# A two-stage kernel whose three compute engines keep the program's order, with time mixing placed by hand between the products and fewer PSUM banks for each use

## The chip, the cores and the metric

The kernel runs on one core of one Trainium2 chip. The core has a matrix engine (TensorE, PE in the profile), a vector engine (VectorE, DVE), a scalar engine (ScalarE, ACT), a general engine (GpSimd, POOL) and a queue that issues the loads and stores (SyncE, SP). Each takes its instructions in the order of its own queue and waits at an instruction whose inputs or buffers are not ready. The metric is the device time of one execution in microseconds (us); the lower, the better.

## The reference

An attention block with a decaying state for 4 batches, 8 heads, 768 steps and 48 features a head, and then a gated feed-forward block on its 3072 x 384 output:

```python
for t in range(S):
    kt, vt, rt = (k[:, :, t], v[:, :, t], r[:, :, t])
    cur = np.einsum('bhd,bhe->bhde', u[None] * kt, vt)
    y[:, :, t] = np.einsum('bhd,bhde->bhe', rt, state + cur)
    state = w[None, :, :, None] * state + np.einsum('bhd,bhe->bhde', kt, vt)
...
rms = np.sqrt(np.mean(x * x, axis=-1, keepdims=True) + 1e-06)
xn = x / rms * rms_g
g = xn @ w_gate
silu = g * (1.0 / (1.0 + np.exp(-g)))
val = xn @ w_val
return (silu * val @ w_out).astype(np.float32)
```

d_model is 384 and d_ff is 1536; inputs are float32, the weights arrive as 64-bit words.

## The kernel before, in words

The 768 steps are cut into 12 chunks (`s`) of 64 steps; a chunk holds 256 tokens, 64 of each batch. Two kinds of work are done for every chunk.

**Time mixing** (lines 290 to 423) computes the attention of one chunk from the state that the chunk before left. In the order of `mixing(s)`: `prep_r` scales r and k by the tables of powers of w on DVE (ME from chan, then chan itself) and copies half of ME to MO on ACT. `prep_u` multiplies r, k and u and sums them to `du` on DVE (three instructions on TOK). `diagonal(s, half)` writes `du` times a diagonal mask into ME and MO: 16 small ACT instructions for a half, two DVE instructions for chunk 0 (lines 315 to 328). `prep_k` makes KH on DVE and then issues the next chunk's TOK load. `scores(s, half)` is 16 small matmuls into `pa` and two masked DVE copies from it; the second half issues the next chunk's chan load. `outputs(s, half)` is 24 small matmuls into `py`, then squares (`sq`) and a scaled copy (`yT`) on ACT. `states(s, half)` is 16 small matmuls into `pu` and four ACT copies into VS, and then the next load of VS. `normalise(s)` is one matmul into `pm`, the square root on ACT (with a load of its function table), the reciprocal on DVE, and two products (`xa`, `xb`) with an ACT copy of each to the other half of the partitions. The last chunk has no `states`.

**The feed-forward block** has a first form for chunks 0 and 1 and a second for the other ten. In the first form (here called the first layer), `gate_val(s, nn)` (line 447) computes one of 12 slices of 128 gate and value columns with two calls of `product`, each six matmuls (line 434), then Silu on ACT and a DVE product give `h`; `add_cell(s, q, j)` (line 465) multiplies three slices with the output weights and adds to a sum. While this runs, the weights are loaded in 24 pieces and rounded from 64-bit words: `round_piece` (line 173) has one ACT instruction, two DVE and one on POOL for each, and three load buffers.

In the second form, two chunks are taken as a pair (`s` = 2, 4, 6, 8, 10). `weight_sums` and `token_sums` make sums and differences (DVE), and `group(s, m)` (line 562) computes two slices for both chunks with seven products instead of eight, in PSUM banks a, b and c, each of two halves; the second product of a pair needs the token sum t2. Six groups make a pair's `h`. `project(s, j)` (line 611) then multiplies with the output weights: four times 12 matmuls, one ACT copy and two stores each.

**The check** (line 538) loads the weights a second time in 48 parts, with one buffer (`again`), and looks on ACT for values that the rounding could not represent: two ACT instructions each (`mag`).

**What sets the order.** The program text interleaves lists of steps with the helper `alongside`: so many time-mixing steps after so many product steps. But the order of the text is only a priority there. The framework's scheduler sorts each engine's instructions by its own estimate of when inputs will be ready, for all five queues. PSUM has eight banks: six for `a`, `b`, `c` (two each), one for time mixing (`at`), one for `po`, the sums of `add_cell` and `project`; chunk 0's mixing borrows a, b and c in turn.

## Time and profile before

| what | us |
|---|---|
| median of three runs | 821.41 |
| lowest of the three | 817.68 |
| the profiled execution | 818.58 |
| its span, first to last instruction | 816.7 |
| PE busy | 684.9 |
| DVE busy | 407.8 |
| ACT busy | 354.1 |
| POOL busy | 47.6 |

The highest of the three runs took 3746.5 us. A table row of the profile reads: line, engine, operation, output<-inputs, shapes, count | busy us in all, mean ns of one | idle time of the engine just before these instructions, and what ended it. A row of waits reads: who waited for whom, us in total, times, the longest. A row of the chain of waits reads: start, duration, what. In a table of stages each engine has its busy time and, in brackets, its instructions; PEclk is the clock that TensorE was granted, as a share of full speed; a matmul in float32 stands in the records as two. A row of the timeline reads: start, duration, engine, line, operation, count.

### The profile page before, as it was taken

What the parts mean: (1) busy time and instruction counts of PE and PEld (TensorE: products, weight loads), DVE (VectorE), ACT (ScalarE), POOL (GpSimd) and SP (SyncE); (2) the same over time, 40 slices, a digit from 0 to 9 for tenths busy, and PEclk for the clock granted to TensorE, in tenths of its full rate; (3) what the DMA queues carried; (4) which work ended last, traced back from release to release, by engine and by line L of the source; (5) the groups of instructions that cost most, each with busy time, mean ns of one, the idle gap of its engine ahead of it and who ended that gap; (6) DMA issues with size and microseconds to landing.
All of it is one profiled execution on the core that took longest, in us unless ns stands there. A gap on an engine that the chain in (4) does not pass through costs nothing.

```text
span 816.7 us, 14933 instructions
## 1 busy us (share of the span) xinstructions
PE 684.9 (84%) x6326; PEld 513.0 (63%) x6326; DVE 407.8 (50%) x575; ACT 354.1 (43%) x955; POOL 47.6 (6%) x40
## 2 busy tenths in 40 slices
PE   2484875887767778799997999997999999999996
PEld 2353653655546556665875766875668877578853
DVE  6999671341354235633656526565437654325510
ACT  3673933853583356235255173273262471321200
POOL 5444220000000000000000000000000000000000
PEclk9887898889898889899998999998999999999999
DMA  8767623353533342023022023210230210000000
GB/s 229 213 196 231 194 70 87 83 142 91 120 114 107 87 112 73 1 51 92 10 41 74 16 44 91 41 44 31 50 92 10 41 35 2 20 20 1 2 21 22
DMA packets 20572, 61.32 MB, mean 75 GB/s; under 512 B 3984, under 2 KB 7056, under 8 KB 19344
## 3 DMA queue, kind: packets, MB, share of 16 engines
q1 hardware_dynamic: 20496, 60.28, 28.0%
q8 instruction: 51, 0.84, 0.4%
q14 instruction: 25, 0.20, 0.1%
HBM read 55.54 MB, written 4.72 MB: 74 GB/s over the span
## 4 chain that ended last, share of the span: by engine, by line
PE 47%; DMA 19%; DVE 14%; ACT 13%; issue 3%; POOL 2%; SPq 0%; ACTq 0%; DVEq 0%; POOLq 0%
PE po L621 18%; PE b L439 10%; PE a L439 6%; PE c L439 6%; DMA again<-in_wka_dram 5%; DMA again<-in_wot_dram 4%; DMA again<-in_wkb_dram 4%; DMA chan<-in_chan_dram 4%; ACT ME L328 3%; PE pa L337 2%; ACT mag L547 2%; DMA TOK<-in_tok_dram 2%; ACT MO L328 1%; DVE rms L418 1%; PE py L361 1%
## 5 line engine op out<-in xcount | busy, mean ns | idle before, releaser
L621 PE MATMUL po<-wo,h 128*128 128x384 f32 x480 | 163.1, 493 | 2.8 <-ACT o L629 2.8
L621 PEld LDWEIGHTS po<-wo,h 128*128 128x128 f32 x480 | 88.6, 190 | 63.3 <-ACT o L629 4.9
L439 PE MATMUL b<-t,wb 64*128 64x256 f32 x360 | 49.1, 407 | 19.3 <-DVE gv L589 19.3
L547 ACT ACTIVATE mag<-again 128x288 f32<-128x288 f32 x48 | 22.2, 463 | 94.7 <-DMA again<-in_wka_dram 34.3
L328 ACT ACTIVATE MO<-dmask,du 64x64 f32<-64x64 f32 x176 | 48.3, 338 | 25.8 <-PE py L366 25.2
L471 PE MATMUL po<-wo,h 128*128 128x384 f32 x96 | 43.5, 590 | 16.6 <-DVE o L476 7.2
L439 PE MATMUL gv<-xa,wa 64*128 64x256 f32 x288 | 47.2, 436 | 11.7 <-ACT MO L328 7.5
L439 PE MATMUL c<-t,s 64*128 64x256 f32 x360 | 49.7, 399 | 8.0 <-DVE gv L604 8.0
L439 PEld LDWEIGHTS b<-t,wb 64*128 64x128 f32 x360 | 37.0, 201 | 25.4 <-DVE gv L589 20.9
L439 PE MATMUL b<-xa,wa 64*128 64x256 f32 x360 | 47.9, 398 | 5.2 <-DVE gv L582 5.0
L439 PE MATMUL a<-xa,wa 64*128 64x256 f32 x360 | 49.3, 389 | 3.5 <-DVE h L595 3.5
L361 PE MATMUL py<-ME,VS 128*64 128x64 f32 x288 | 39.8, 242 | 14.4 <-issue 8.6
L439 PE MATMUL b<-t,s 64*128 64x256 f32 x360 | 49.6, 395 | 0.4 <-DVE t L558 0.4
L629 ACT COPY o<-po 128x384 f32<-128x384 f32 x20 | 9.6, 478 | 92.5 <-PE po L621 83.9
L439 PE MATMUL c<-xb,s 64*128 64x256 f32 x360 | 47.9, 400 | 0.7 <-DVE gv L590 0.5
L439 PEld LDWEIGHTS c<-t,s 64*128 64x128 f32 x360 | 37.7, 197 | 15.1 <-DVE gv L604 9.5
L361 PEld LDWEIGHTS py<-ME,VS 128*64 128x64 f32 x288 | 31.4, 153 | 24.9 <-issue 17.4
L439 PEld LDWEIGHTS gv<-xa,wa 64*128 64x128 f32 x288 | 32.5, 211 | 21.2 <-issue 12.5
L439 PE MATMUL a<-xb,wb 64*128 64x256 f32 x360 | 45.4, 384 | 0.0
L337 PE MATMUL pa<-ME,chan 48*64 48x64 f32 x384 | 31.1, 240 | 16.7 <-DVE MO L342 15.1
L328 ACT ACTIVATE ME<-dmask,du 64x64 f32<-64x64 f32 x176 | 44.8, 331 | 0.6
L589 DVE TENSOR_TENSOR gv<-b,m 128x512 f32<-128x512 f32 x30 | 20.7, 692 | 48.4 <-PE b L439 48.3
(120 smaller groups left out, 1324.2 us busy)
## 6 DMA issues: line engine op xcount, KB each, us to landing
TOK<-in_tok_dram SPq DMA_DIRECT2D x12, 768.0 KB, 5.5
chan<-in_chan_dram SPq DMA_DIRECT2D x24, 384.0 KB, 6.1
VS<-in_vpad_dram SPq DMA_DIRECT2D x24, 336.0 KB, 4.9
raw<-in_wka_dram SPq DMA_DIRECT2D x8, 576.0 KB, 5.3
raw<-in_wkb_dram SPq DMA_DIRECT2D x8, 576.0 KB, 6.1
raw<-in_wot_dram SPq DMA_DIRECT2D x8, 576.0 KB, 4.7
again<-in_wka_dram SPq DMA_DIRECT2D x16, 288.0 KB, 2.7
again<-in_wkb_dram SPq DMA_DIRECT2D x16, 288.0 KB, 2.7
```

The source lines that it names most:

```text
L328: nc.scalar.mul(t[rows, b, p, :], dmask[rows], du[rows, x : x + 1])
L337: nc.tensor.matmul(pa[to, bl, p, :], CH[rows, 1, b, p, :], m[rows, b, p, :], start=True, stop=True, skip_group_check=True,)
L361: nc.tensor.matmul(py[64 * z : 64 * z + 64, i, cols], VS[:, z, b, at : at + L], m[:, b, 3, :], start=True, stop=False, skip_group_check=True,)
L418: nc.vector.reciprocal(rms, rms)
L439: nc.tensor.matmul(ps_[:, z, 0:NT], lhs[rows, cc, :], rhs[rows, cc, :], start=start and cc == 0, stop=cc == CC - 1, skip_group_check=True,)
L471: nc.tensor.matmul(po, h[:, j * P : (j + 1) * P], wo[q][:, o, :], start=o == 0, stop=o == NQ - 1)
L547: nc.scalar.activation(mag, hi, AF.Abs)
L589: nc.vector.tensor_add(gv[:, :, 3], bank["b"][sl], m1)
L621: nc.tensor.matmul(po, h_of[s, m][:, 2 * x + j // 2, at : at + P], wo[i][:, o, :], start=m == 0 and x == 0, stop=m == last and x == 1,)
L629: nc.scalar.copy(osb, po)
```

## The change

1. A small class passes every instruction that `fast` gives to PE, DVE or ACT on with the request that it keep the order of the program; `pe`, `dve` and `act` replace `nc.tensor`, `nc.vector` and `nc.scalar`. SP and POOL are not wrapped. (In the profile of the changed kernel and in its order all of these instructions have the line of the helper, L89.)
2. The steps of time mixing are cut finer, each with a letter: R and K (`decay_r`, `decay_k`), 1, 2, 3 (the three instructions of the bonus), d/D (diagonal, first/second half), a/A (scores), m/M (the masked copies), y/Y (outputs), q (squares), r (`pm` and the root), n (normalise), h/H (KH, one half each; H issues the TOK load), u/U (states). `mix(s, "...")` issues them in the order given.
3. `alongside` is gone: every gate_val, add_cell, rounding and mixing step of the first layer is written out, and in the pairs a table says after which product of which group which steps come. One check stands after the third and one after the sixth product of each group, in all pairs but the first. The weight sums are spread over the first pair's start and its groups; the token sums of a pair come directly after the last normalise.
4. Banks: time mixing has two of its own (`at`), also for chunk 0 and for `ps_wk`. The bank for `po` is gone. gate_val alternates between a and b; add_cell takes c, for both token halves at once; the four projections take a, b, c, b. The tile `o` has two buffers.
5. The first VS load is issued ahead of the first weight pieces; `dmask` is made earlier.

The diff, cut to its core:

```diff
+class InOrder:
+
+
+    def __init__(self, tc, engine):
+        self.tc, self.engine = tc, engine
+
+    def __getattr__(self, name):
+        give = getattr(self.engine, name)
+        return lambda *args, **kwargs: self.tc.keep_in_program_order(give(*args, **kwargs))
...
+    pe, dve, act = (InOrder(tc, engine) for engine in (nc.tensor, nc.vector, nc.scalar))
...
-    ps_at = ctx.enter_context(tc.tile_pool(name="ps_at", bufs=1, space=PSUM))
-    ps_o = ctx.enter_context(tc.tile_pool(name="ps_o", bufs=1, space=PSUM))
+    ps_at = ctx.enter_context(tc.tile_pool(name="ps_at", bufs=2, space=PSUM))
...
+    load_v(0)
     stage()
     stage()
-    load_v(0)
     stage()
...
-    rota = deque("abc")
-
-    def at_tile(shape, name, s):
-
-        if s == 0:
-            rota.rotate(1)
-            return ps_gv.tile(shape, FP32, name=name, tag=rota[0])
+
+    def at_tile(shape, name):
         return ps_at.tile(shape, FP32, name=name, tag="at")
...
+    def decay_r(s):
+
+        dve.tensor_mul(ME, CH[:, 0], free_dims(up, (0, B), (L, HP), (1, L)))
+        act.copy(MO[64:128], ME[64:128])
+
+    def decay_k(s):
+        dve.tensor_mul(CH[:, 1], CH[:, 1], free_dims(down, (0, B), (L, HP), (1, L)))
+
+    def bonus_1(s):
+        dve.tensor_mul(TOK[:, 0], TOK[:, 0], TOK[:, 1])
+
+    def bonus_2(s):
+        dve.tensor_mul(TOK[:, 0], TOK[:, 0], free_dims(utab, (0, B), (D, HP), (1, D)))
+
+    def bonus_3(s):
+
...
+                    act.mul(t[rows, b, p, :], dmask[rows], du[rows, x : x + 1])
+
+    def state_k(s, z):
+
+        if s == NS - 1:
+            return
+        rows = slice(64 - 64 * z, 128 - 64 * z)
+        dve.tensor_mul(KH[rows, z], TOK[rows, 1], free_dims(wk[rows], (0, B), (D, HP), (1, D)))
+        if z == 1:
+            load_tok(s + 1)
+
...
+    def rms(s):
+        pm = at_tile([P, NT], f"pm_{s}")
+        pe.matmul(pm, ones, sq_of[s][:, 0], start=True, stop=True)
+        rms_of[s] = one.tile([P, NT], FP32, name=f"rms_{s}", tag="rms")
+        act.activation(rms_of[s], pm, AF.Sqrt, scale=1.0 / DM, bias=eps)
...
-    h_of, turn = {}, deque("abc")
+    h_of, turn = {}, deque("ab")
...
-    def add_cell(s, q, j):
+    def add_cell(q, s):
 
         rounded(PER_Q * (q + 1))
-        po = ps_o.tile([P, DM], FP32, name=f"po_{s}_{q}_{j}", tag="po")
-        for o in range(NQ):
-            h = h_of[s, q * NQ + o]
-            nc.tensor.matmul(po, h[:, j * P : (j + 1) * P], wo[q][:, o, :], start=o == 0, stop=o == NQ - 1)
+        po = ps_gv.tile([P, 2, 512], FP32, name=f"po_{s}_{q}", tag="c")
+        for j in range(2):
+            for o in range(NQ):
+                h = h_of[s, q * NQ + o]
+                pe.matmul(
+                    po[:, j, 0:DM], h[:, j * P : (j + 1) * P], wo[q][:, o, :], start=o == 0, stop=o == NQ - 1
+                )
         if q == 0:
-            sums[s, j] = work.tile([P, DM], FP32, name=f"o_{s}_{j}", tag="o", bufs=2 * FIRST)
-            nc.scalar.copy(sums[s, j], po)
+            sums[s] = work.tile([P, 2, DM], FP32, name=f"o_{s}", tag="o", bufs=FIRST)
+            act.copy(sums[s], po[:, :, 0:DM])
         else:
-            nc.vector.tensor_add(sums[s, j], po, sums[s, j])
+            dve.tensor_add(sums[s], po[:, :, 0:DM], sums[s])
         if q == WQ - 1:
-            store(sums[s, j], s, j)
-
-    late = deque()
-
-    def cell(q, s):
-        steps = []
-        for o in range(NQ):
-            steps.append(lambda o=o: gate_val(s, q * NQ + o))
-            if late:
-                steps.append(late.popleft())
-        late.extend(lambda j=j: add_cell(s, q, j) for j in range(2))
-        return steps
-
-    def alongside(steps, others, spare=0):
-
-        todo, n = deque(others), len(others)
-        for x, f in enumerate(steps):
+            for j in range(2):
+                store(sums[s][:, j], s, j)
...
+    def mix(s, what):
+
+
+        todo = {
+            "R": decay_r, "K": decay_k, "1": bonus_1, "2": bonus_2, "3": bonus_3, "q": squares, "r": rms,
+            "n": normalise,
+        }
+        halves = {"d": diagonal, "a": scores, "m": masked, "y": outputs, "h": state_k, "u": states}
+        for c in what:
+            if c in todo:
+                todo[c](s)
+            else:
+                halves[c.lower()](s, int(c.isupper()))
+
+    def rounding(k):
+        for _ in range(k):
+            round_piece()
+
+    mix(0, "RK123aAdmyDMY")
+    rounding(2)
+    mix(0, "qr")
+    rounding(2)
+    mix(0, "n")
+    gate_val(0, 0), rounding(1), mix(0, "h")
+    gate_val(0, 1), rounding(1), mix(0, "Hu")
+    gate_val(0, 2), mix(0, "U"), rounding(2)
+    add_cell(0, 0), rounding(2)
+    gate_val(0, 3), mix(1, "12")
+    gate_val(0, 4), mix(1, "3Rd")
+    gate_val(0, 5), mix(1, "K"), rounding(1), mix(1, "aDm"), rounding(1)
+    add_cell(1, 0), mix(1, "AMyY"), rounding(1), mix(1, "qr"), rounding(1), mix(1, "n")
+    gate_val(1, 0), rounding(1), mix(1, "h")
+    gate_val(1, 1), mix(1, "Hu"), rounding(1)
+    gate_val(1, 2), mix(1, "U"), rounding(1)
+    add_cell(0, 1), mix(2, "12")
+    gate_val(1, 3), mix(2, "3Rd")
+    gate_val(1, 4), mix(2, "K")
+    gate_val(1, 5), mix(2, "aDm")
+    add_cell(1, 1), mix(2, "A"), rounding(1), mix(2, "M")
+    gate_val(0, 6), mix(2, "y"), rounding(1)
+    gate_val(0, 7), mix(2, "Y")
+    gate_val(0, 8), mix(2, "q"), rounding(1), mix(2, "r")
+    add_cell(2, 0), mix(2, "n")
+    gate_val(1, 6), mix(2, "hHu"), rounding(1)
+    gate_val(1, 7), mix(2, "U"), rounding(1)
+    gate_val(1, 8), mix(3, "12")
+    add_cell(2, 1), mix(3, "3Rd"), rounding(1)
+    gate_val(0, 9), mix(3, "K"), rounding(1)
+    gate_val(0, 10), mix(3, "aDm")
+    gate_val(0, 11), rounding(1), mix(3, "AM")
...
+    add_cell(3, 0), mix(3, "h")
+    gate_val(1, 9), mix(3, "yH")
+    gate_val(1, 10), mix(3, "Y"), sum_1(0)
+    gate_val(1, 11), mix(3, "q"), sum_2(0), mix(3, "r")
+    add_cell(3, 1), mix(3, "nuU")
+    token_sum(2, 1), token_sum(2, 2)
 
     for s in range(FIRST, NS, 2):
+        first_block, n = s == FIRST, s + 2
+        fill = {}
+        if first_block:
+            fill.update({(0, 0): lambda: (token_sum(s, 3), sum_3(0)), (0, 1): lambda: (token_sum(s, 4), sum_4(0))})
+            fill.update({(1, 0): lambda: sum_1(1), (2, 0): lambda: sum_2(1), (2, 1): lambda: sum_4(1)})
+            fill.update({(2, 4): lambda: sum_3(1)})
+        if n < NS:
+            plan = {
+                (0, 2): "R", (1, 1): "K", (1, 4): "1", (2, 0): "2", (2, 2): "3d", (3, 0): "h", (3, 2): "aDm",
+                (4, 0): "H", (4, 2): "AM", (4, 4): "y", (5, 2): "Y", (5, 4): "q", (5, 5): "u",
+            }
         else:
+            plan = {}
+        for m in range(NN // 2):
+            steps = group(s, m)
+            for k, f in enumerate(steps):
+                f()
+                if (m, k) in fill:
+                    fill[m, k]()
+                if (m, k) in plan:
+                    mix(n, plan[m, k])
+                if not first_block and k in (2, 5):
+                    check()
+        if n == NS:
+            for j in range(4):
+                project(s, j, False), project(s, j, True)
+            break
+        mix(n, "U"), mix(n + 1, "R12")
+        project(s, 0, False), mix(n, "r"), mix(n + 1, "3K")
+        project(s, 0, True), mix(n + 1, "ad"), mix(n, "n")
+        project(s, 1, False), mix(n + 1, "ADmh")
+        project(s, 1, True), mix(n + 1, "yMH")
+        project(s, 2, False), mix(n + 1, "Yq")
+        project(s, 2, True), mix(n + 1, "r")
+        project(s, 3, False), mix(n + 1, "un")
+        project(s, 3, True), mix(n + 1, "U")
+        for x in (1, 2, 3, 4):
+            token_sum(n, x)
...
+    po_of = {}
+
+    def project(s, j, second):
+
+        if not second:
+            po_of[s, j] = ps_gv.tile([P, DM], FP32, name=f"po_{s}_{j}", tag="abcb"[j])
+        po = po_of[s, j]
...
```

More of the change, by code (lines that the diff above doesn't have):

```diff
@@ new lines, in run @@
+    def run(*steps):
+        for f in steps:
+            f()
+    def mix(s, what):
[9 more added lines that the diff above has]
+                halves[c.lower()](s, int(c.isupper()))
@@ L605, in seventh @@
[L605 to L607 removed]
+            dve.tensor_add(gv[:, :, 1], bank["c"][sl], gv[:, :, 1])
+            act.activation(gv[:, 0, 1], gv[:, 0, 1], AF.Silu)
+            dve.tensor_mul(h[:, 2:4], gv[:, 0, 2:4], gv[:, 1, 2:4])
+            dve.tensor_mul(h[:, 1], gv[:, 0, 1], gv[:, 1, 1])
         return [first, second, third, fourth, fifth, sixth, seventh]
[L611 to L632 removed]
@@ new lines, in project @@
+    def project(s, j, second):
+        if not second:
+            po_of[s, j] = ps_gv.tile([P, DM], FP32, name=f"po_{s}_{j}", tag="abcb"[j])
+        po = po_of[s, j]
+        last = NN // 2 - 1
+        for m in range(3, 6) if second else range(3):
+            for x in range(2):
+                i, o = divmod(m + x * NN // 2, NQ)
+                at = (j % 2) * P
+                pe.matmul(
+                    po, h_of[s, m][:, 2 * x + j // 2, at : at + P], wo[i][:, o, :],
+                    start=m == 0 and x == 0, stop=m == last and x == 1,
+                )
+        if second:
+            osb = work.tile([P, DM], FP32, name=f"o_{s}_{j}", tag="o", bufs=FIRST)
+            act.copy(osb, po)
+            store(osb, s + j // 2, j % 2)
```

234 lines of the change are left out of this document (78 added, 156 removed).

## The prediction

> **What bounds the kernel now.** I read the page's head first, then busy time by stage, then what TensorE (PE) waited for in each stage, then the chain of waits and the durations of single instructions.
>
> ```profile
> span 816.7 us, 14933 instructions
> ```
>
> The profiled execution took 818.58 us, so 1.9 us lie around the span. The median of the runs, 821.41, stands 2.8 above it. Busy time by stage, cut where PE's work changes (first product of the first layer at 40.1, its last matmul at 250.2, then each pair of chunks):
>
> ```profile
> core 0: us, PE busy (x) PEld busy (x) DVE busy (x) ACT busy (x) POOL busy (x), PEclk, DMA share, GB/s
> 0.00:40.10 40.10, 12.45 (x231) 11.25 (x231) 31.94 (x59) 19.34 (x52) 19.32 (x21) 0.93 0.83 224
> 40.10:250.20 210.10, 154.39 (x1374) 109.86 (x1375) 112.92 (x141) 118.16 (x326) 28.28 (x19) 0.86 0.48 133
> 250.20:388.30 138.10, 114.03 (x1034) 84.64 (x1034) 58.59 (x85) 62.49 (x181) 0.00 (x0) 0.91 0.28 72
> 388.30:502.10 113.80, 106.42 (x1055) 80.59 (x1054) 60.88 (x85) 49.95 (x136) 0.00 (x0) 0.97 0.19 48
> 502.10:616.85 114.75, 107.60 (x1055) 81.47 (x1054) 60.97 (x85) 50.07 (x136) 0.00 (x0) 0.97 0.19 48
> 616.85:722.25 105.40, 103.53 (x995) 78.25 (x994) 52.96 (x76) 38.91 (x95) 0.00 (x0) 1.00 0.10 23
> 722.25:810.50 88.25, 86.50 (x596) 66.92 (x596) 29.50 (x49) 14.75 (x30) 0.00 (x0) 1.00 0.04 10
> 810.50:816.70 6.20, 0.00 (x0) 0.00 (x0) 0.00 (x0) 0.46 (x1) 0.00 (x0) 0.70 0.15 37
> ```
>
> The late pairs are PE-bound: 103.53 busy in 105.40 at clock 1.00. The loss is early: PE idles 56 us in 40.1 to 250.2 and 24 in the next stage, and its clock there is 0.86 and 0.91. Of the waits, the first three are PE's between 40 and 250, the fourth PE's in the whole run; then what ScalarE (ACT) waited for at the weight check:
>
> ```profile
> PE pa L337 <- DVE MO L342: 15.1, 3, 7.4
> ...
> PE gv L439 <- ACT MO L328: 7.5, 1, 7.5
> ...
> PE pu L395 <- ACT VS L403: 5.6, 2, 3.2
> ```
> ```profile
> PE b L439 <- DVE gv L589: 19.3, 4, 6.4
> ```
> ```profile
> L547 ACT ACTIVATE mag<-again 128x288 f32<-128x288 f32 x48 | 22.2, 463 | 94.7 <-DMA again<-in_wka_dram 34.3 <-DMA again<-in_wot_dram 34.1 <-DMA again<-in_wkb_dram 26.3
> ```
>
> All 48 checks stand early in ACT's queue, with one buffer, and ACT sits 94.7 us in front of a load that starts only when the check before is read. The Silu behind it is late, then VectorE (DVE), then PE.
>
> **The price list.** From the chain of waits (a product, a projection half of six matmuls, the same product after a long idle, the square root's table load and the root); DVE; ACT; DMA landings:
>
> ```profile
> 34.42 1.28 ACT L417
> ...
> 35.72 0.48 ACT rms L417
> ```
> ```profile
> 436.21 4.42 DMA TOK<-in_tok_dram
> ...
> 447.70 2.93 PE b L439 x12
> ...
> 454.87 1.29 PE c L439 x12
> ...
> 462.42 4.07 PE po L621 x12
> ```
> ```profile
> L190 DVE SCALAR_TENSOR_TENSOR bits<-raw,bits 128x576 int32<-128x576 int32 x24 | 25.6, 1068 | 0.5
> L418 DVE RECIPROCAL rms<-rms 128x256 f32<-128x256 f32 x12 | 21.0, 1750 | 20.7 <-ACT rms L417 20.7
> L310 DVE TENSOR_TENSOR KH<-TOK,wk 64x768 f32<-64x768 f32 x22 | 20.9, 952 | 29.6 <-PE pu L395 29.1
> ...
> L295 DVE TENSOR_TENSOR chan<-chan,down 128x1024 f32<-128x1024 f32 x12 | 14.7, 1223 | 29.7 <-DMA chan<-in_chan_dram 29.7
> ...
> L456 DVE TENSOR_TENSOR h<-gv,h 128x256 f32<-128x256 f32 x24 | 10.1, 422 | 66.6 <-ACT h L455 66.5
> ```
> ```profile
> 36.09 3.91 ACT L328 ACTIVATE MO<-dmask,du 64x64 f32<-64x64 f32 x16
> ```
> ```profile
> L294 ACT COPY MO<-ME 64x1024 f32<-64x1024 f32 x12 | 12.5, 1042 | 0.8 <-DVE ME L293 0.4
> ...
> L455 ACT ACTIVATE h<-gv 128x256 f32<-128x256 f32 x24 | 8.9, 371 | 0.7 <-PE gv L439 0.5
> ```
> ```profile
> again<-in_wka_dram SPq DMA_DIRECT2D x16, 288.0 KB, 2.7
> ```
>
> So 16 diagonal multiplies in one piece hold ACT for 3.9 us. ME has chan's shape (1.2); xa, xb and the token sums have KH's columns (0.95); a copy of 768 columns is 0.8 by MO's 1.04 for 1024. A restart after an idle of several us costs 2.93 - 1.29 = 1.64.
>
> **The change, part by part.** First, ACT in the first layer. Before, checks (mag) stand between the Silus (h) of chunk 0:
>
> ```order
> L455 ACTIVATE h_0_785<-gv_0_772 128x256
> L547 ACTIVATE mag_2527<-again_2525 128x288
> L548 ACTIVATE mag_2527,seen<-mag_2527 128x288
> L455 ACTIVATE h_1_822<-gv_1_809 128x256
> L547 ACTIVATE mag_2550<-again_2548 128x288
> ```
>
> After, no check stands there, but a chunk's diagonal is one piece ahead of a Silu:
>
> ```order
> L89 ACTIVATE h_4_534<-gv_4_521 128x256
> L89 COPY MO<-ME 64x1024
> L89 ACTIVATE ME<-dmask,du_537 64x64 x8
> L89 ACTIVATE MO<-dmask,du_537 64x64 x8
> L89 ACTIVATE h_5_570<-gv_5_557 128x256
> ```
>
> What moved: the checks go to the groups of the last four pairs (after products 3 and 6, so 3.9 or 5.2 us apart, against 2.7 for a landing and some 0.6 around it: no wait left), and h_5 now stands behind 16 multiplies. On DVE, `chan<-chan,down` stands behind h_5, and the scores need chan.
>
> Stage 1, to the first product: the same chain, without two KH and the roundings that stood between: 40.1 becomes 38.
>
> Stage 2, the first layer. PE's work at full clock: 24 gate_val of two products, 24 x 2.58 = 62; 8 add_cell, 8 x 4.07 = 33; mixing. One mixing is read from the pair at 616.85: 103.53, less 42 products (54) and 8 halves (33), leaves 16.5 for two that lack one chunk's states, so some 9; three, and chunk 0's states (2), are 29. Sum 124. Its stalls, walked through the new order:
> - scores of chunk 1: ME 1.2, MO 1.0, diagonal 3.9, Silu 0.4, h 0.4, chan 1.2 in a row, 8.1, with one gate_val (2.6) of cover less 2 lost at its start: 7. Chunks 2 and 3 have two gate_vals: 5 each. Sum 17.
> - states: KH (two of 0.95) and a rounding (two steps, the longer 1.07, so up to 2.1) stand on DVE behind h, which itself waits for the Silu: 5, 4, and 7 for chunk 2, whose xa and xb copies and two table loads stand ahead of that Silu. Sum 16.
> - weights just in time: gate_val 3 waits for a raw load issued behind VS (some 5), add_cell 1 for a rounding behind the masks (5). Sum 10.
> - xa of chunk 1 is used at once: squares, pm, 1.28 + 0.48, reciprocal 1.75, two of 0.95, copy 0.8: 7.5. Chunk 2's pm: 1.5. Sum 9.
> - restarts: about nine of these exceed 3 us: 9 x 1.64 = 15.
> That is 67, so 191 in place of 207.5 (to the second layer's first product, 2.6 of which lie before 250.2). Stage 2 ends at 229, before at 247.6. Two banks for gate_val instead of three cost nothing: the bank comes back after two gate_vals, 5.2 us, and Silu and h take 0.8; if a diagonal stands there, it is in the stalls above. add_cell as one tile moves as many columns.
>
> Stage 3, first pair: before 388.3 - 247.6 = 140.7, most of it checks. A full pair's work is 103.5 + 1.9 = 105.4. Added: the second product waits for t2 behind chunk 3's reciprocal (4) and restarts (1.6); eight weight sums in the groups' DVE, 1.4 each by KH's 0.95 for 768 columns of their 1152, of which I leave 2.5 uncovered; the diagonal (below). Sum 115.
>
> Stage 4, three pairs. At the pair's start DVE, first before, then after (t is the token sum that the second product needs, TOK the next chunk's load):
>
> ```order
> L422 TENSOR_TENSOR xb_2459<-yT_2340,rms_2455 64x768
> L300 TENSOR_TENSOR TOK<-TOK 128x768
> L557 TENSOR_TENSOR t_4_2470<-xa_2458,xa_2113 128x768
> L301 TENSOR_TENSOR TOK<-TOK,utab 128x768
> L558 TENSOR_TENSOR t_4_2471<-xb_2459,t_4_2470 128x768
> ```
> ```order
> L89 TENSOR_TENSOR xb_2421<-yT_2329,rms_2389 64x768
> L89 TENSOR_TENSOR t_4_2459<-xa_2420,xa_2243 128x768
> L89 TENSOR_TENSOR t_4_2461<-xb_2421,t_4_2459 128x768
> L89 TENSOR_TENSOR xa_2420<-xb_2421,xa_2420 128x768
> L89 TENSOR_TENSOR t_4_2464<-xb_2244,t_4_2461 128x768
> ```
>
> What moved: TOK, a wait for a DMA, leaves the front of t. Before, the wait for TOK (436.21) starts a chain that ends in one of b's four waits (4.8 each on the mean) and the slow product at 447.70; after, chunk s+3 is normalised during the last 8 us of projections, and that covers reciprocal, xa, xb, copies and t (6.5). If that cover failed, each pair would pay 4. Remaining: in group 2, du (0.95) after the second product's add, 3.9 of diagonal and a check (mag's 0.46 and a second pass, about 1.1) stand ahead of Silu a, which ends at 10.4 where the next group wants bank a at 9.1: 1.4; group 3 and the DMAs of TOK and chan, which now meet check loads, 1. So 108, 108, and 106 for the pair without the last states.
>
> Stage 5: 88.3 as before (checks take 2.2 of ACT's 9.1 us a group), tail 6.2.
>
> Sum: 229 + 115 + 108 + 108 + 106 + 88.3 + 6.2 = 760.5 of span, 762 as profiled. I say 760 for the median.
>
> The Trainium skill ("ScalarE: Activation LUTs", What ACT_TABLE_LOAD costs) gives a switch of table 1.38 us of drain behind the 1.28 of the load. The rows above show 1.30 from the load's start to the root's, so no drain; by the page, four switches on the first layer's path would add 5.5, and the sum would be 766.
>
> **Unknown costs.** The order of SP and POOL stays the scheduler's. Bounds for a stall in the first layer: 0 where DVE and ACT run ahead, up to the 7.5 of the worst wait before; with ten of them, 0 to 75; the walk's 52 without restarts is nearer the upper, because the members are added in a row. For a pair's diagonal: 0 to the full 3.9 plus a restart, twice, 11; I take 2.4, as the walk leaves little of it uncovered.
>
> **Rivals.**
> - *Cover holds nearly everywhere.* First layer at 124 + 30, pairs at 107, 105, 105, 104: 38 + 154 + 107 + 105 + 105 + 104 + 94.5 = 708. For it: DVE and ACT are busy only 113 and 118 of 210 there. Against: in order, the length of the chain counts, not the sum.
> - *Given back.* First layer as long as before (247), pairs at 118, 113, 114, 111, then 94.5: 798. For it: PE's waits there were for the mask and the state copies, which the diagonal burst now delays. Against: no ACT wait for checks.
> - *Slower.* One mechanism: each of 22 bursts (two a chunk, chunks 1 to 11) holds a Silu whose bank PE needs. Work and known ends without stalls are 38 + 124 + 3 x 105.4 + 103.5 + 94.5 = 676; before is 141 above, so from 6.4 us a burst it is slower than before. The bare chain, 8.1 + 1.64, would give 676 + 22 x 9.7 = 890. Against: in the groups two to three products of 1.29 and PE's scores lie beside it.
> - *The change doesn't do what it says.* The order shows PE, DVE and ACT as written, so I give it nothing.
>
> **How the numbers follow.** Forecast (735 to 785) 0.58, cover holds 0.17, given back 0.19, slower 0.06. The range 716 to 803 takes in about half of the first rival and most of the second, and leaves out some 0.19. About 2% can be told from no change here: below 805 faster, above 838 slower. Of given back, 0.11 is faster and 0.08 same: faster 0.86, same 0.09, slower 0.05.
>
> **What would show it.** Right: no idle of ACT before mag (94.7 now); the wait b <- L589 at a pair's start gone (19.3); the second layer's first product near 229; pairs at 108 and clock 1.00; PE waiting in the first layer for chan (scores), KH (states), xa, weights. Wrong: the first layer ends later than 240, or a Silu's bank holds PE for over 3 us in each pair, or check loads hold ACT in the groups.

## The result, and the profile after

The changed kernel takes 749.12 us (median of 4 runs, 748.61 to 749.56) against 820.67 for the kernel before on the same chip: a ratio of 0.9139, 95% interval 0.9112 to 0.9166. The prediction was 760, with a range of 716 to 803.

The profiled execution took 749.56 us. Its head, and the busy time by stage, cut as before (first product of the first layer, first product of each pair; the last stretch ends 1.3 us behind the last projection):

```profile
span 747.5 us, 14896 instructions
```
```profile
core 0: us, PE busy (x) PEld busy (x) DVE busy (x) ACT busy (x) POOL busy (x), PEclk, DMA share, GB/s
0.00:39.10 39.10, 10.67 (x166) 9.64 (x166) 26.47 (x48) 10.94 (x18) 14.40 (x20) 0.86 0.73 187
39.10:231.70 192.60, 145.65 (x1417) 108.84 (x1416) 88.86 (x123) 80.70 (x216) 30.67 (x20) 0.83 0.35 96
231.70:344.10 112.40, 105.68 (x1058) 80.07 (x1054) 73.57 (x97) 50.35 (x140) 0.00 (x0) 0.98 0.21 50
344.10:448.25 104.15, 103.01 (x1056) 79.52 (x1053) 60.88 (x85) 58.02 (x170) 0.00 (x0) 1.00 0.35 87
448.25:552.20 103.95, 102.84 (x1058) 79.56 (x1054) 60.85 (x85) 58.12 (x170) 0.00 (x0) 1.00 0.34 87
552.20:654.20 102.00, 100.89 (x992) 78.02 (x990) 59.38 (x83) 56.63 (x165) 0.00 (x0) 1.00 0.28 73
654.20:741.30 87.10, 85.90 (x603) 66.92 (x602) 30.30 (x53) 26.65 (x66) 0.00 (x0) 1.00 0.18 47
```

From the first layer's first product to the start of the second pair it was 388.3 - 40.1 = 348.2 us before and is 344.1 - 39.1 = 305.0 now: 43 of the 69 us of span. The three middle pairs give 9.7, 10.8 and 3.4. The pairs are now all but full of PE work at clock 1.00; the first layer is not: 46.9 us idle, clock 0.83, lower than before (0.86). What PE waits for:

```profile
PE pa L89 <- issue: 18.2, 3, 7.4
...
PE pu L89 <- DVE KH L89: 13.2, 6, 6.0
...
PE pm L89 <- DVE sq L89: 6.8, 4, 1.8
PE a L89 <- DVE h L89: 4.7, 4, 1.3
PE gv L89 <- DVE xa L89: 4.4, 1, 4.4
PE b L89 <- DVE t L89: 3.7, 1, 3.7
PE gv L89 <- POOL wb L204: 3.1, 2, 2.2
...
PE po L89 <- POOL wo L204: 2.6, 2, 2.0
```

The scores (`pa`) of chunks 1 to 3 are the largest from the first product on, although no engine is named. The timeline at the first of them tells who it was:

```profile
75.19 1.21 DVE L89 TENSOR_TENSOR ME<-chan,up 128x1024 f32<-128x1024 f32 x1
...
76.44 1.04 ACT L89 COPY MO<-ME 64x1024 f32<-64x1024 f32 x1 [2.48 <-DVE ME L89]
77.51 1.99 ACT L89 ACTIVATE ME<-dmask,du 64x64 f32<-64x64 f32 x8
79.52 2.02 ACT L89 ACTIVATE MO<-dmask,du 64x64 f32<-64x64 f32 x8
81.44 0.36 ACT L89 ACTIVATE h<-gv 128x256 f32<-128x256 f32 x1
...
81.83 0.42 DVE L89 TENSOR_TENSOR h<-gv,h 128x256 f32<-128x256 f32 x1 [5.42 <-ACT h L89]
82.17 1.22 DVE L89 TENSOR_TENSOR chan<-chan,down 128x1024 f32<-128x1024 f32 x1
...
83.49 0.34 PE L89 MATMUL pa<-ME,chan 48*64 48x64 f32 x1 [7.38 <-issue]
```

Each step begins where the one before ends, across three queues: the Silu (`h`) is behind the diagonal on ACT, `h` on DVE behind the Silu, `chan` behind `h`, and PE stands still from 76.12. No single instruction is slow.

ACT in front of a check waits far less than the 94.7 us of before, in all 48 places together:

```profile
L89 ACT ACTIVATE mag<-again 128x288 f32<-128x288 f32 x48 | 22.3, 465 | 18.2 <-DMA again<-in_wka_dram 7.7 <-DMA again<-in_wot_dram 6.7 <-DMA again<-in_wkb_dram 3.6
```

### The profile page after: what moved, and what is told of

It is laid out like the page before. It is cut to its first block, busy times and chain, and to the rows that moved or that the text cites. A ratio compares the mean times of both kernels' runs of the same rounds, so it can differ in the third digit from the quotient of the medians.

```text
span 747.5 us, 14896 instructions
## 1 busy us (share of the span) xinstructions
PE 654.6 (88%) x6326; PEld 502.6 (67%) x6326; DVE 400.3 (54%) x569; ACT 341.4 (46%) x945; POOL 45.1 (6%) x40
## 4 chain that ended last, share of the span: by engine, by line
PE 77%; DVE 10%; ACT 5%; issue 4%; DMA 2%; POOL 1%; DVEq 0%; POOLq 0%; ACTq 0%
PE po L89 25%; PE b L89 14%; PE a L89 9%; PE gv L89 9%; PE c L89 8%; PE py L89 5%; PE pa L89 4%; PE pu L89 3%; DVE bits L89 2%; DVE gv L89 1%; ACT MO L89 1%; DMA chan<-in_chan_dram 1%; DVE rms L89 1%; DVE TOK L89 1%; DVE h L89 1%
## 5 line engine op out<-in xcount | busy, mean ns | idle before, releaser
L89 PE MATMUL po<-wo,h 128*128 128x384 f32 x576 | 199.4, 499 | 2.6 <-POOL wo L204 2.6
L89 PEld LDWEIGHTS po<-wo,h 128*128 128x128 f32 x576 | 108.6, 193 | 73.9 <-POOL wo L204 3.9
L89 DVE TENSOR_TENSOR gv<-b,m 128x512 f32<-128x512 f32 x90 | 62.1, 690 | 64.3 <-PE b L89 63.6
L89 PE MATMUL pa<-ME,chan 48*64 48x64 f32 x384 | 31.1, 240 | 32.3 <-issue 18.2
L89 PEld LDWEIGHTS pa<-ME,chan 48*64 48x64 f32 x384 | 27.9, 152 | 41.8 <-issue 39.6
L89 ACT ACTIVATE gv<-gv 128x512 f32<-128x512 f32 (+1 forms) x60 | 31.1, 519 | 48.7 <-DVE gv L89 48.7
L89 PE MATMUL gv<-xa,wa 64*128 64x256 f32 x288 | 47.6, 464 | 4.4 <-DVE xa L89 4.4
L89 DVE TENSOR_TENSOR h<-gv,h 128x256 f32<-128x256 f32 x24 | 10.2, 424 | 74.8 <-ACT h L89 74.7
L89 DVE TENSOR_TENSOR gv<-c,gv 128x512 f32<-128x512 f32 x60 | 41.4, 690 | 15.4 <-PE c L89 14.3
L89 ACT ACTIVATE ME<-dmask,du 64x64 f32<-64x64 f32 x176 | 43.8, 330 | 12.1 <-DVE du L89 11.6
L89 PE MATMUL a<-xa,wa 64*128 64x256 f32 x360 | 45.1, 383 | 4.7 <-DVE h L89 4.7
L89 PE MATMUL b<-t,s 64*128 64x256 f32 x360 | 45.4, 386 | 4.0 <-DVE t L89 3.7
L89 PE MATMUL b<-xa,wa 64*128 64x256 f32 x360 | 45.5, 385 | 0.6 <-DVE gv L89 0.6
L89 PE MATMUL b<-t,wb 64*128 64x256 f32 x360 | 44.5, 379 | 0.8 <-DVE gv L89 0.8
L89 ACT ACTIVATE MO<-dmask,du 64x64 f32<-64x64 f32 x176 | 44.4, 335 | 0.4
L89 PE MATMUL c<-xb,s 64*128 64x256 f32 x360 | 44.3, 378 | 0.0
L89 PEld LDWEIGHTS py<-ME,VS 128*64 128x64 f32 (+1 forms) x576 | 36.4, 136 | 11.3 <-issue 10.7
L89 PE MATMUL c<-t,s 64*128 64x256 f32 x360 | 43.9, 376 | 0.0
L89 PE MATMUL a<-xb,wb 64*128 64x256 f32 x360 | 43.9, 376 | 0.0
L89 PE MATMUL gv<-xb,wb 64*128 64x256 f32 x288 | 40.1, 407 | 3.1 <-POOL wb L204 3.1
L89 PE MATMUL py<-ME,VS 128*64 128x64 f32 (+1 forms) x576 | 39.9, 229 | 2.5 <-DVE MO L89 2.5
L89 PEld LDWEIGHTS gv<-xa,wa 64*128 64x128 f32 x288 | 32.7, 227 | 13.7 <-DVE xa L89 4.8
```

What stands on the lines that cost most here:

```text
L89: return lambda *args, **kwargs: self.tc.keep_in_program_order(give(*args, **kwargs))
```

## The experiments

Theory A: the kernel gains because the scheduler had put the checks early in ACT's queue, and the order of the program keeps them late. Theory B: what gains is the placement of mixing by hand. The medians in us, and where the time lies (from the timeline: first product of the first layer; from there to the start of the second pair; pairs 2, 3, 4; the last pair to its last projection):

| kernel | median | first product | to pair 2 | pairs 2, 3, 4 | last |
|---|---|---|---|---|---|
| before | 817.3 to 820.8 | 40.1 | 348.2 | 113.8, 114.8, 105.3 | 88.3 |
| before, no checks | 757.69 | 41.0 | 284.3 | 114.6, 113.6, 105.6 | 88.3 |
| before, checks kept late | 781.29 | 40.5 | 287.2 | 123.9, 125.7, 108.4 | 88.3 |
| before, in order | 833.50 | 42.4 | 319.6 | 126.9, 130.3, 116.2 | 88.3 |
| changed | 749.12 | 39.1 | 305.0 | 104.2, 103.9, 102.0 | 85.8 |
| changed, no checks | 746.73 | 39.4 | 304.1 | 102.7, 102.7, 100.8 | 85.8 |
| changed, scheduler | 810.51 | 33.0 | 349.8 | 112.1, 110.9, 109.3 | 85.8 |
| changed, scheduler, checks kept late | 754.03 | 33.3 | 284.6 | 114.6, 113.3, 113.3 | 85.8 |
| changed, scheduler in the first layer | 714.75 | 33.6 | 275.2 | 103.9, 103.9, 102.0 | 85.8 |
| the same, PE in order throughout | 719.30 | 33.1 | 281.7 | 103.9, 103.9, 102.0 | 85.8 |
| the same, only DVE in order in the pairs | 732.57 | 33.3 | 279.7 | 109.0, 109.1, 107.3 | 85.8 |
| changed, mixing earlier by hand | 734.95 | 39.8 | 292.4 | 103.9, 103.9, 102.0 | 85.8 |
| changed, diagonal on DVE | 737.09 | 38.2 | 296.8 | 102.8, 102.8, 100.9 | 85.8 |
| scheduler in the first layer, diagonal on DVE | 706.80 | 34.4 | 273.5 | 102.8, 102.8, 100.9 | 85.8 |

**1. The kernel before without its checks.**

```diff
-    parts = [(src[i], k) for i in range(WQ) for src in (wka, wkb, wot) for k in range(PIECE // CHECK)] if wide else []
+    parts = []
```

> The kernel before with its 48 checks left out: no second load of the weights, no mag instructions; the count of values that could not be rounded is taken as zero. Theory A (the gain is that the checks leave the first layer and the first pair): these two stages took 207.5 and 140.7 us before and 192.6 and 112.4 after, so without any check the kernel before should lose about those 14.9 + 28.3 = 43 us and come to some 778; the three middle pairs stay at 113.8, 114.75 and 105.4. Theory B (the hand placement of mixing is the gain; the checks only fill idle time of ACT): 94.7 us of waiting in front of mag cost little, and the time stays at 805 or more.

757.69 us, ratio 0.923 (0.9195 to 0.9266). Theory A holds, and the checks cost more than it said: 63 us, all of it before the second pair (348.2 becomes 284.3). Its stages before the second pair, PE idle 26.6 us in the first layer where the changed kernel idles 46.9:

```profile
41.00:203.50 162.50, 135.86 (x1342) 99.55 (x1342) 103.30 (x129) 86.12 (x227) 28.41 (x19) 0.91 0.40 109
203.50:325.30 121.80, 110.43 (x1063) 81.78 (x1062) 67.48 (x94) 49.85 (x136) 0.00 (x0) 0.97 0.20 50
```

The first layer is 30 us shorter than the changed kernel's. Some of that is work behind the mark: in run 1, 8 matmul records of add_cell and 64 of the states run after the second layer's first product, in the changed kernel none. To the second layer's first fifth product (216.3 and 242.3 us) the lead is 26 us. That was not expected, and the later runs ask why. The middle pairs do not gain, and the waits of b for DVE stay at their 19.3 us.

**2. The changed kernel without its checks** (the same edit; in both, the count at the end is then taken as zero).

> The changed kernel with its 48 checks left out. Theory A: in their new places the checks lie under the products; mag waits 18.2 us in all, but no wait of PE names it: 747 to 749. Rival C (a check behind the diagonal's 16 multiplies is what holds the Silu of bank a in group 2, and the loads of the checks meet those of TOK and chan): the four waits a <- DVE h (4.7 us in all) go, and the time is 743 to 745.

746.73 us, ratio 0.9102 (0.907 to 0.9134). The time is theory A's but for 0.3 us, the detail rival C's. Of the four waits of a for h one is left, 1.3 us in the first pair, which never had a check. Pairs 2 to 4 lose 1.5, 1.2 and 1.2; 1.7 us of that come back between the last projection and the end. The checks cost 2.4 us in the changed kernel's late places and 63 in the early ones of before.

**3. The changed text, sorted by the scheduler.**

```diff
-        return lambda *args, **kwargs: self.tc.keep_in_program_order(give(*args, **kwargs))
+        return give
```

> The changed kernel with the same text, the same banks and the same places of every step, but PE, DVE and ACT sorted by the framework's scheduler again. The checks then stand early in ACT's queue, in the first layer and the first pair, as in the kernel before. Theory A: the first layer and the first pair are as long as before or nearly so, 795 to 815. Theory B (placement in the text and the second bank for mixing are the gain, the scheduler would respect them): 750 to 765.

810.51 us, ratio 0.9881 (0.9843 to 0.9919), as theory A had it. The checks are early again (114 to 313 us), and 348.2 is 349.8. Text and banks without the order are worth 10 us.

**4. The kernel before, in order.**

```diff
+    pe, dve, act = (InOrder(tc, engine) for engine in (nc.tensor, nc.vector, nc.scalar))
```
(and `pe.`, `dve.`, `act.` in place of `nc.tensor.`, `nc.vector.`, `nc.scalar.`)

> The kernel before, its text, banks and evenly spread steps unchanged, but PE, DVE and ACT keep the order of the program. The checks stand in the last four pairs. Theory A (that the checks are late is most of the gain): the first layer and first pair give back most of 43 us, the spread text costs some stalls of its own: 780 to 800. Theory B (the placement by hand is the gain, order without it makes chains of mixing stand in PE's way): 821 or more, since each step of mixing then stands directly behind the one it needs.

833.5 us, ratio 1.0171 (1.0128 to 1.0214). Theory B's number (821 or more) was met and theory A's (780 to 800) was not: the part to the second pair gains 28.6 us, but each middle pair loses 11 to 16. With this text, which was not written for it, order loses more in the pairs than the late checks bring.

**5. The kernel before, only the checks kept late.**

```diff
+    act = InOrder(tc, nc.scalar)
...
-        nc.scalar.activation(mag, hi, AF.Abs)
-        nc.scalar.activation(mag, mag, AF.Relu, scale=-(2.0**15), bias=1.0, accum_out=seen[:, n : n + 1])
+        act.activation(mag, hi, AF.Abs)
+        act.activation(mag, mag, AF.Relu, scale=-(2.0**15), bias=1.0, accum_out=seen[:, n : n + 1])
```

> The kernel before with one thing added: the two ACT instructions of a check keep their place in the program behind the ACT instruction written ahead of them; everything else on all engines stays with the scheduler, and text and banks are those of before. Theory A (all that the check costs comes from its early places): the 757.7 us of the kernel before without checks, and the 2.4 that the checks cost the changed kernel (749.1 less 746.7): about 760. Rival D (the check's loads, one behind the other through a single buffer, hold the loads of TOK and chan on the queue of SP wherever the checks stand): 775 or more. Theory B (placement of mixing by hand): 805 or more.

781.29 us, ratio 0.9547 (0.9519 to 0.9574): rival D's number (775 or more), but not by the way that it named. Pinning 96 of ACT's instructions brings 36.7 us, more than half of what leaving them out brings. The rest goes in the pairs, 9.3, 12.1 and 2.8 longer than without checks. What DVE waits for in the groups, first without the checks, then with them late, the same two lines of the program (L595 is L607 in the second text, L606 is L618):

```profile
DVE h L606 <- ACT gv L600: 18.8, 27, 0.7
DVE h L595 <- ACT gv L594: 18.6, 26, 1.9
```
```profile
DVE h L607 <- ACT gv L606: 39.8, 29, 4.4
...
DVE h L618 <- ACT gv L612: 23.4, 27, 2.6
```

A check now delays ACT's Silus in the groups: 26 us more of waiting for them, against 5 more in DVE's waits for the loads of TOK (12.4 and 16.4) and chan (29.1 and 30.1), which rival D had named. ACT still sits 53.9 us in front of the 48 checks, waiting for their loads, where the changed kernel sits 18.2. So late is not enough: where the checks stand among the products counts too.

**6. The changed text, scheduler, only the checks kept late.**

```diff
-    pe, dve, act = (InOrder(tc, engine) for engine in (nc.tensor, nc.vector, nc.scalar))
+    pe, dve, act = nc.tensor, nc.vector, nc.scalar
+    late = InOrder(tc, act)
...
-        act.activation(mag, hi, AF.Abs)
-        act.activation(mag, mag, AF.Relu, scale=-(2.0**15), bias=1.0, accum_out=seen[:, n : n + 1])
+        late.activation(mag, hi, AF.Abs)
+        late.activation(mag, mag, AF.Relu, scale=-(2.0**15), bias=1.0, accum_out=seen[:, n : n + 1])
```

> The changed kernel, its text and banks, with PE, DVE and ACT sorted by the scheduler, but for the two ACT instructions of a check, which keep their place. Theory A: from the 810.5 us of the freely sorted text the early checks' cost goes; that text's first layer and first pair took 206.6 and 143.2 us, and without checks in them I expect 165 (the kernel before without checks had 162.5) and 112: 738. Theory B (order by hand is worth more than that outside the checks): the first layer stays at 190 or more, or the pairs at 110, and it takes 755 or more.

754.03 us, ratio 0.9215 (0.9193 to 0.9237): 16 above theory A, a microsecond below theory B. Two kept instructions a check are worth 56.5 us here. Theory A is nearer on the first layer (33.3 to 206.1 is 172.8; 165 expected) and wrong on the pairs, which stay at 113 to 115: their gain is the order's, not the checks'. DVE 11 us into the second pair shows what the scheduler does there:

```profile
320.82 0.69 DVE L619 TENSOR_TENSOR gv<-b,m 128x512 f32<-128x512 f32 x1 [0.94 <-PE b L452]
327.13 0.96 DVE L307 TENSOR_TENSOR TOK<-TOK 128x768 f32<-128x768 f32 x1 [5.62 <-DMA TOK<-in_tok_dram]
...
329.00 0.68 DVE L626 TENSOR_TENSOR gv<-b,m 128x512 f32<-128x512 f32 x1
```

The add of L626 frees bank b. It was sorted behind a product that waits 5.62 us for a load, and PE waits 5.14 us for it. The kernel before has such a row 59 us into its second pair, with a reciprocal, xa and xb in it as well, and PE waits 5.77 us there:

```profile
440.66 0.96 DVE L300 TENSOR_TENSOR TOK<-TOK 128x768 f32<-128x768 f32 x1 [2.09 <-DMA TOK<-in_tok_dram]
...
442.53 1.75 DVE L418 RECIPROCAL rms<-rms 128x256 f32<-128x256 f32 x1
...
445.96 0.96 DVE L422 TENSOR_TENSOR xb<-yT,rms 64x768 f32<-64x768 f32 x1
446.95 0.69 DVE L589 TENSOR_TENSOR gv<-b,m 128x512 f32<-128x512 f32 x1
```

**7. The changed kernel, its first layer left to the scheduler.**

```diff
     def __getattr__(self, name):
         give = getattr(self.engine, name)
+        if not InOrder.on:
+            return give
...
+    InOrder.on = True
     add_cell(3, 0), mix(3, "h")
```

> The changed kernel, with the order of the program kept only from the last two add_cells and the pairs on; the first layer's PE, DVE and ACT are sorted by the scheduler, with no check among them, since the checks are pinned to the pairs. Theory E (in the first layer, the order by hand is worse than the scheduler's: the kernel before without checks reached the second layer's first fifth product at 216.3 us, the changed one at 242.3): the first layer loses 15 to 26 us, all pairs stay at 112, 104, 104, 102: 723 to 735. Rival F (the scheduler was quick there because it had three banks in turn for gate_val and chunk 0's mixing in them; with a and b alone it is not): 742 or more.

714.75 us, ratio 0.8747 (0.8727 to 0.8767): 34 us below the changed kernel, and 8 below theory E's range (723 to 735): its direction, by more than it said. The first pair is 1.1 us shorter than the changed kernel's, the others are the same to 0.3; 5.5 us are gained to the first product and 28.7 in the first layer. Of these 28.7, 20.7 are idle time of PE and 7.9 busy time, at a clock of 0.91 for 0.83. Rival F falls: a and b alone are enough for gate_val. The scores of chunks 1 to 3 wait no longer. The scheduler starts their steps much earlier: for chunk 1 the product that makes `chan` ends 32 us ahead of the scores, for chunks 2 and 3 22 and 32 us, where in the changed kernel it ends 0.1 us ahead of them:

```profile
36.91 1.21 DVE L307 TENSOR_TENSOR chan<-chan,down 128x1024 f32<-128x1024 f32 x1
...
70.06 0.27 PE L354 MATMUL pa<-ME,chan 48*64 48x64 f32 x1
```

The largest wait of PE in the first layer's products is now another:

```profile
PE po L488 <- DVE h L472: 16.4, 5, 6.5
```

**8. The diagonal on DVE in all chunks.**

```diff
-            if s == 0:
+            if True:
                 dve.tensor_mul(
```

> The changed kernel, with the diagonal of every chunk as two DVE products of 0.69 us for a half in place of 16 ACT multiplies of 0.33. Theory (the burst on ACT is what the scores of chunks 1 to 3 and bank a of group 2 wait for): the three waits of the scores (7.4, 4.8, 6.0) lose 2.5 to 3.9 each, the four waits of a for h (4.7 in all) go: 735 to 740. Rival G (DVE, in order too, takes the place of ACT: 2.8 us a chunk ahead of the products and sums that the banks wait for): 748 to 755.

737.09 us, ratio 0.902 (0.9 to 0.9041), as the theory had it: the three score waits fall from 18.2 to 10.1 us in all, the waits of a for h are gone, and pairs 2 to 4 lose 1.4, 1.1 and 1.1. DVE has room for it: it was busy 61 us of a pair's 104.

**9. The mixing steps earlier by hand, in order.** One of the three places:

```diff
-    gate_val(0, 2), mix(0, "U"), rounding(2)
+    gate_val(0, 2), mix(0, "U"), rounding(2), mix(1, "RK")
     count = w_range()
-    add_cell(0, 0), rounding(2)
-    gate_val(0, 3), mix(1, "12")
-    gate_val(0, 4), mix(1, "3Rd")
-    gate_val(0, 5), mix(1, "K"), rounding(1), mix(1, "aDm"), rounding(1)
+    add_cell(0, 0), rounding(2), mix(1, "12")
+    gate_val(0, 3), mix(1, "3d")
+    gate_val(0, 4), mix(1, "D")
+    gate_val(0, 5), rounding(1), mix(1, "am"), rounding(1)
```

> The changed kernel, order kept everywhere, with only the first layer's text changed: R and K of chunks 1 to 3 stand one to three gate_vals earlier (K no longer behind the Silu that the diagonal holds), the bonus and the diagonal one gate_val earlier, and the diagonal's two halves apart. Theory H (the scores of chunks 1 to 3 wait because their steps stand in one row close ahead of them, and moving the row forward in the same order cures it): the three waits of 7.4, 4.8 and 6.0 us go, with the slow products behind them (2.06 for 1.15 and some gate_vals of 2.79 for 2.58) about 24 us: 722 to 730. Rival J (the first layer is limited by DVE and ACT in order, KH, roundings and Silus; the wait only moves from the scores to gate_val and states): 738 or more.

734.95 us, ratio 0.8978 (0.8949 to 0.9008): between the two. The waits of 4.8 and 6.0 us (chunks 2 and 3) are gone, but for 1.8 us in which po waits for h. Chunk 1's 7.4 went over to the next thing that was late, the rounded weights (2.6 and 3.1 us before the edit):

```profile
PE po L89 <- POOL wo L204: 7.1, 3, 5.2
...
PE gv L89 <- POOL wb L204: 4.3, 2, 3.7
```

**10. As 7, with PE in order in the first layer too.**

```diff
-        if not InOrder.on:
+        if not InOrder.on and self.engine is not self.tc.nc.tensor:
```

> As the run with the first layer left to the scheduler (714.75 us), but PE keeps the order of the program in the first layer too; only DVE and ACT are sorted by the scheduler there. Theory H (what costs 34 us is where the mixing instructions stand on DVE and ACT): the scheduler starts them earlier here too, so 715 to 725. Rival K (PE's own order costs it: scores stand ahead of gate_vals that could run): 740 to 749.

719.3 us, ratio 0.8785 (0.8755 to 0.8815). Of the 34 us, PE's own order costs 4.5; some 30 are the places of the instructions on DVE and ACT, as theory H says.

**11. Runs 7 and 8 together.**

> The two gains together: first layer left to the scheduler (714.75 us), and the diagonal as DVE products in all chunks (737.1 in place of 749.1 with the first layer in order, of which the four pairs gave 0.8, 1.4, 1.1 and 1.1 and the rest came from the first layer). If the first layer's gain there was cover for scores that the scheduler gives already: 714.75 less 4.4, 709 to 712. If the diagonal's ACT time still counts in the first layer: under 707. Rival G (DVE, with 2.8 us more a chunk, holds h in the first layer, whose waits of po for h are 16.4 us already): 714 or more.

706.8 us, ratio 0.8636 (0.8608 to 0.8664), the fastest of the study, 42 us below the changed kernel. The median is the second theory's (under 707), the profile speaks for the first: the part to the second pair gains another 1.7 and the middle pairs 1.1 each, less than in run 8. The two profiled executions, 713.98 and 709.24, differ by 4.7 us, which is the first theory's 4.4. But the first is the fastest of its four and the second the slowest of its four; the medians differ by 8, and where the other 3 lie no profile shows. So the record does not decide between the two.

**12. As 7, but of the pairs' engines only DVE in order** (and the checks).

```diff
-        if not InOrder.on:
+        if not InOrder.on or self.engine is not self.tc.nc.vector:
```

> As the run with the first layer left to the scheduler (714.75 us; its pairs 111.3, 103.9, 103.9, 102.0, 85.8), but in the pairs only DVE keeps the order of the program, and of ACT only the checks; PE and the rest of ACT are sorted by the scheduler there too. With nothing but the checks kept, the pairs of the changed text took 111.8, 114.6, 113.3, 113.3, 85.8, and in each of the three middle pairs one wait of b for DVE stands, 4.5 to 5.1 us with a slow product behind it: before the add that frees bank b, the scheduler had put a wait for TOK, a reciprocal, xa and xb on DVE. Theory L (the pairs' gain is DVE's order alone: that row of mixing is no longer ahead of the add): pairs at 103.9 to 106, 715 to 722. Rival M (PE and ACT must keep their places too, since the products that cover each step are then no longer beside it): pairs at 109 or more, 732 or more.

732.57 us, ratio 0.8949 (0.8925 to 0.8974): rival M. The waits of b for DVE are gone from the middle pairs, but now a waits 3.4 us for h in each. The granted clock is 0.50 behind that wait, for two products and not one (344.01 to 349.29 in the second pair, 2.93 and then 2.77 us):

```profile
344.00:346.70 2.70, 2.69 (x12) 2.20 (x14) 1.75 (x3) 2.67 (x10) 0.00 (x0) 0.50 0.00 0
346.70:349.30 2.60, 2.60 (x15) 2.04 (x13) 1.47 (x3) 0.59 (x3) 0.00 (x0) 0.50 0.36 113
```

ACT at that place, here and then in the changed kernel:

```profile
336.01 1.99 ACT L345 ACTIVATE ME<-dmask,du 64x64 f32<-64x64 f32 x8 [2.35 <-DVE du L92]
338.02 2.02 ACT L345 ACTIVATE MO<-dmask,du 64x64 f32<-64x64 f32 x8
...
341.34 1.75 ACT L345 ACTIVATE ME<-dmask,du 64x64 f32<-64x64 f32 x7
343.12 0.39 ACT L645 ACTIVATE gv<-a 128x256 f32<-128x256 f32 x1
```
```profile
367.29 1.99 ACT L89 ACTIVATE ME<-dmask,du 64x64 f32<-64x64 f32 x8 [2.35 <-DVE du L89]
369.29 2.02 ACT L89 ACTIVATE MO<-dmask,du 64x64 f32<-64x64 f32 x8
...
372.15 0.36 ACT L89 ACTIVATE gv<-a 128x256 f32<-128x256 f32 x1
```

The scheduler draws half of the second diagonal ahead of the Silu of bank a, 7.1 us after the burst began in place of 4.9. So the pairs need ACT's order as well as DVE's; whether they need PE's too this run does not tell apart, since PE was sorted by the scheduler as well.

## Why the prediction was right, point by point

The change taken apart, with medians: text and banks alone 820.7 to 810.5 (-10.2); the checks kept late, to 754.0 (-56.5); the order kept in the pairs, to 714.75 (-39.3); the order kept in the first layer, to 749.1 (+34.4). The runs are from several chips, on which the kernel before takes 817.3 to 820.8, so each step is known to some 3 us. Of the -39.3, some 31 lie in the three middle pairs and 8.9 in the first layer (172.8 to 163.9): in run 6 the scheduler had put weight sums and mixing steps of chunk 4 there, and ACT had a fourth chunk's diagonal. The prediction had their sum; it did not see that one part of the change loses.

- *What bounds it.* The early checks: right, 63 us by run 1. But the 19.3 us of b <- L589 were wrongly tied to a pair's start and to t. In pairs 2 to 4 of before they lie 54 to 59 us into the pair; the one whose rows stand under run 6 is behind TOK, the reciprocal, xa and xb. They are gone as forecast, because DVE's order no longer allows that row: in run 12, with DVE alone in order, they are gone too. "No wait left" in front of the checks was too strong: their loads still hold ACT for 18.2 us in the groups, and by run 2 the checks cost 2.4 in all.
- *Stage 1.* 38 forecast, 39.1 measured. Left to the scheduler it is 33.6 with the same text.
- *Stage 2.* 191 forecast, 192.6 measured. Of the 52 us of stalls the scores were 17 (18.2 measured), the states 16 (13.2), the weights 10 (3.1 + 2.6 = 5.7), xa and pm 9 (4.4 and, for chunks 1 to 3, 5.2); PE idles 46.9. Its busy time is 145.65 against 124 + 15 with restarts. A restart was priced at 1.64, one slow product; run 12 shows two (2.93 and 2.77 us at a clock of 0.50), and the products of gate_val take 80.8 us here for the 62 at full clock. That these 7 us too many and the 5 too few of the stalls all but cancel is luck. What the walk missed is not a size: it took the row of steps as given. Run 7, in which the scheduler starts the same steps earlier, has 28.7 us less; with PE in order (run 10) 22.2 of them stay, and moving the steps by hand (run 9) brings 11.6. The 207.5 us of before end at 247.6, which the prediction calls the second layer's first product; that product starts at 238.5 there, so by the same mark the first layer of before has 198.4 and the first pair 149.7. The forecast does not rest on it, and the two together are the same.
- *Two banks for gate_val cost nothing*: right; no wait of gv for h stands among the changed kernel's, and run 7, with two banks, has a first layer of 163.9 with all of its work in it, against 162.5 in run 1 with three and some of the work behind the mark.
- *Stage 3.* 115 forecast, 112.4 measured: the wait for t 4 (3.7), the diagonal 1.4 (1.3).
- *Stage 4*, the term that was mis-sized: 108, 108, 106 forecast, 104.15, 103.95, 102.0 measured, 12 of the 13 us by which the sum of 760.5 lies above the span of 747.5. The pair's work was taken as 105.4: PE's busy time of 103.53 in a pair of before, plus 1.9 for the states that this pair lacks. That busy time was not all work: the same pair has 100.89 here (552.20 to 654.20), 2.6 less, and run 8, with the diagonal off ACT, has 102.8 for a full pair. What made these 2.6 stays open. The other two terms, 1.4 for the diagonal and 1 for the checks, are not additive: either run that takes one of them away removes the same wait, 1.1 to 1.5 a pair.
- *Stage 5.* 94.5 with the tail forecast, 93.3 measured. The projections had waited for their one bank in before; with banks a, b, c, b all runs have 85.8 for 88.3. Before has three such waits in the last pair, 1.6 of these 2.5 us; two of them:

```profile
785.28 8.01 PE L621 MATMUL po<-wo,h 128*128 128x384 f32 x24 [0.45 <-ACT o L629]
793.86 8.01 PE L621 MATMUL po<-wo,h 128*128 128x384 f32 x24 [0.57 <-ACT o L629]
```

- *Rivals.* "Cover holds nearly everywhere" (708) did not happen; run 11 comes to 706.8, but with another order and with the diagonal on DVE, so that the two numbers meet is luck. "Given back" (first layer to 247) failed for the whole and was right in kind: the order loses in the first layer, of which the burst that it named has 7.3 us (run 8: 185.2 for 192.6). "Slower": the burst was priced at 6.4 us for break-even; moving all 22 bursts to DVE gains 12.0, or 0.55 each.
- *The table load.* The Trainium skill ("ScalarE: Activation LUTs", What ACT_TABLE_LOAD costs) gives a drain of 1.38 us beside the load. This trace shows none on either side: the load starts within 0.02 us of the end of the instruction before it, and the root starts 1.30 after the load does. So the sum without it was the right one:

```profile
101.25 1.28 ACT L89 ACT_TABLE_LOAD   x1
102.55 0.47 ACT L89 ACTIVATE rms<-pm,eps 128x256 f32<-128x256 f32 x1
```

## What to carry to other kernels

An instruction of no importance early in a queue that runs in order can cost more than any product: look for an engine that waits long at work nobody needs yet, and pin that work first. Here, keeping the program's order paid in the pairs, where each step stands a whole chain of steps ahead of its use and beside enough work to cover it; in the first layer, where the text puts the chain's steps in one row in front of their user, the scheduler did better by 34 us. Order by hand can be kept for one stretch and left to the scheduler for another, and the two are worth measuring apart.

## What the runs showed of the hardware

The same DVE instruction of the rounding takes 0.74 or 1.84 us. From run 7, DVE and then POOL (start, duration):

```profile
67.14 0.74 DVE L205 SCALAR_TENSOR_TENSOR bits<-raw,bits 128x576 int32<-128x576 int32 x1
...
68.28 1.84 DVE L205 SCALAR_TENSOR_TENSOR bits<-raw,bits 128x576 int32<-128x576 int32 x1
```
```profile
68.02 1.48 POOL L208 TENSOR_TENSOR wa<-bits,ulp 128x576 int32<-128x576 int32 x1 [1.46 <-DVE bits L205]
```

The long one starts while an add runs on POOL and ends 0.62 us after it; the short one lies in a gap of POOL (66.56 to 68.02). It is so in the traces of all 14 kernels: of 336 such instructions, 90 take 1.62 to 1.85 us, and each of them starts 0.26 to 0.48 us into an add on POOL and ends 0.61 or 0.62 after it. The other 246 take 0.74 to 0.76, and only one of them starts during an add; in 27 an add starts while they run, and they are not longer for it. So a rounding step costs DVE up to 1.1 us more where it starts behind POOL's add. No run moved one of the two on purpose.
